# Token blocks 3 and 4 of the first MLP computed as a Strassen pair; the planned order extended through the first stage of the second MLP

## Chip, cores and metric

One core of a Trainium2 chip runs the whole program. The metric is device time in microseconds (us) of one execution, the median of the runs shown; beside it stands one execution under the profiler, from which all durations come.

## The reference

```python
q_s = softmax of q over its last axis; k_s = softmax of k over the sequence
kv = einsum('bhsd,bhse->bhde', k_s, v)          # 8 batches, 8 heads, 576 positions, width 64
x  = einsum('bhsd,bhde->bhse', q_s, kv)         # -> 4608 tokens x 512
x  = relu(x @ w_in) ** 2 @ w_out                # first MLP, 512 -> 2048 -> 512
out = (silu(x @ w_gate) * (x @ w_val)) @ w_out2 # second MLP, 512 -> 1536 -> 512
```

q, k and v are float32; the five weight matrices come as float64 and are turned into float32 words on the chip. Every product is made from two-part operands (a rounded part and the rest), three matmuls of 128x128 by 128x512 for one (`mm3`, line 104, whose matmul is line 107).

## The kernel before

The 4608 tokens are nine blocks of 512, numbered 0 to 8. **Direct blocks** (0 to 4, `NE = 5`) go through the first MLP with all eight quarter products of a block matrix product: 16 slices of the hidden width, each four `mm3` into a bank `ph`, the square of the relu, and four `mm3` into banks `acc`: 128 `mm3`, 384 matmuls a block. **Pairs** of blocks, here (5,6) and (7,8), use a seven-product Strassen scheme (`PRODUCTS`) in which the two blocks are the two halves of the rows: 672 matmuls a pair, in two halves, each of two `in_part`s (first weight) and one `out_part` (second weight). The sums on the operand side cost VectorE (DVE) and ScalarE (ACT) work that direct blocks do not have. The second MLP uses the same scheme in `groups` of two blocks (0,1), (2,3), (4,5), (6,7) and a half-width one for block 8: `gated` (504 matmuls a group) and then `out_stage` (252).

**Weight operands.** Pairs and groups read sums of weight quarters from DRAM (`hd`, `ad` for the first MLP; `gvd`, `od` for the second), 512 KB a load, through five slots (`Stream`; line 891 is the load). Two generators, `lane_one` and `lane_two`, make them: 16 "first sets" from words already converted (`first_sets`), then 18 "second sets" (`second_sets`): six gate, six val, then six out, each with two loads of 512 KB, the conversion of two halves (lines 399 to 409), quarter sums (line 334), and stagings (`staged`; line 297 on ACT, line 299 on DVE) with stores at line 326 of seven quarters of 256 KB. Quarters that need no sum are copied from the direct blocks' operands (`first_copies`, 48 stores).

**Attention** of block i, head pair hp is one unit (`kv_unit`, `q_unit`); from block 2 on its result goes to DRAM (`x1d`, store at line 731) and is loaded by `x_unit` (direct) or `bring` (pairs). There are 28 units from block 2 on.

**Order.** Block 0 follows a list written out by hand. Then `Plan`, a list scheduler with a cost for each step, writes every engine's instruction order: a step has an engine, a duration, needs, slots that it takes and frees, and a rank; where several could start on an engine, the lowest rank goes first. Ranks: tails of parts 0 to 0.9, chunks 1, operands `bring` 1.2, attention 2, matmuls of the main line (`direct`, `pair_main`) 3, stores and loads set aside by the lanes (`aside`) 4.9, the lanes 5, copies 6. Attention's unit j may start at 4 + 16j (k, v) and 12 + 16j (q) of planned time (`PACE = 16.0`). The plan runs to the end of the pairs, until the operands of the first group and all second sets are planned; behind it come the eight banks of the second MLP and its ordinary program order, in which each load into a slot is issued from SyncE (SP) when the matmuls ask for the slot.

Of the kernel before, what the change touches and what calls it, by code (L numbers as in the profile page):

```python
# [22 lines left out]
def tile_linear_attention_two_mlps(  # L23
# [45 lines left out]
    ps_a = st_att.enter_context(tc.tile_pool(name="ps_a", bufs=2, space=PSUM))  # L69
# [21 lines left out]
    NE = 5  # L91
# [104 lines left out]
    class Plan:  # L196
# [45 lines left out]
        def run(self, until):  # L242
            while not all(x in self.done for x in until):
# [18 lines left out]
        def finish(self, rank):  # L262
            for u in self.units:
                if u[0] == rank:
                    for _ in u[1]:
                        pass
# [6 lines left out]
    def aside(steps):  # L273

        if prep["plan"]:
            plan.unit(steps, 4.9, plan.now)
        else:
            yield from steps

    made = set()  # L280
    prep = {"n": 0, "issue": nc.sync, "plan": True}

    def aside(steps):

        if prep["plan"]:
            plan.unit(steps, 4.9, plan.now)
        else:
            yield from steps

    made = set()  # L290
    prep = {"stages": [(stp, "wst")] + [(raws, "raw0"), (raws, "raw1")], "raws": [], "n": 0, "r": 0}
    prep.update(issue=nc.sync, plan=True, last={})
# [8 lines left out]
    def staged(place, source, dests, by_rows=False, free=(), key=None):  # L301
# [3 lines left out]
        prep["n"] += 1  # L305
        keep = (tag, prep["n"])
# [16 lines left out]
        def put():  # L323
            yield step("SP", 0.6 * k_, done, (), [keep], [key] if key else (), 4.0)
            for j, to in enumerate(dests):
                prep["issue"].dma_start(to, f32(t[0][:, j]))

        yield from aside(put())
# [29 lines left out]
    class Lane:  # L358


        def __init__(self, halves, raw, stages):
            self.halves, self.raw, self.stages = halves, raw, stages
            self.n = 0

# [4 lines left out]
        def load(self, s, x):  # L369
            kind, f = s  # L370
            tag, tile_ = self.halves[x]
            yield step("SP", 0.6, (), [(tag, s)] if tag else (), (), [("ld", s, x)], 4.0)
            self.loaded[s, x] = tile_()
            nc.sync.dma_start(self.loaded[s, x], w1d[kind[:-1]][f][:, x])
# [5 lines left out]
        def load_raw(self, s, x):  # L380
# [4 lines left out]
            yield step("SP", 0.8, (), [keep], (), [("ld", s, x)], 4.5)  # L385
# [28 lines left out]
        def first_sets(self):  # L414
# [3 lines left out]
            while s:  # L418
# [12 lines left out]
                for x, (source, names) in enumerate(todo):  # L431
# [4 lines left out]
                    if more and self.halves[1][0]:  # L436
                        yield from aside(self.load(more, x))
                if more and not self.halves[1][0]:
                    yield from aside(self.load_two(more))
                made.add(s)  # L440
# [3 lines left out]
        def second_sets(self):  # L444
# [4 lines left out]
            while s:  # L449
                kind, f = s  # L450
# [3 lines left out]
                yield from aside(self.load_raw(s, 1))  # L454
# [15 lines left out]
                if more:  # L470
                    yield from aside(self.load_raw(more, 0))
# [12 lines left out]
                made.add(s)  # L484
# [24 lines left out]
    def lane_two():  # L509
# [6 lines left out]
        lane = Lane(  # L516
            [("qs", q_spare), ("qs", q_spare)], "raw1",
            [slot(qtp, "qT1"), ("kvs", lambda: kv_slot)],
        )
        yield from lane.second_sets()  # L520

    lanes = [lane_one(), lane_two()]
    work = (x for steps in lanes for x in steps)
# [118 lines left out]
    def kv_unit(j, i, hp):  # L642
        me = ("kv", j)
        yield step("SP", 0.7, [("kt.", j - 1)] + ([("x", 1, 3)] if j == 1 else []), [("kt", j)], (), [("kt.", j)], 3.5, True)
# [47 lines left out]
    def v_unit(j, i, hp):  # L692
        yield step("SP", 1.2, (), [("vt", j)], (), [("vt.", j)], 4.0)
        load_v(i, hp)

    def q_unit(j, i, hp):
        n = len(list(runs(i)))
        needs = [("qs.", j - 1)] + ([("ld", 0, 1, "b21")] if j == NP * NE else [])
        yield step("SP", 1.2 * n, needs, [("qs", j)], (), [("qs.", j)], 3.5, True)
# [26 lines left out]
        if hp % 2:  # L726
            nc.vector.tensor_copy(e, px)
        else:
            nc.scalar.copy(e, px)
        yield step("SP", 0.6, (), (), [("e", me)], [("x1", i, hp)], 4.0)  # L730
        nc.sync.dma_start(x1d[i][:, hp], e)

    def q_rest(i, hp, slot, j):

        me = ("pq", i, hp)
        yield step("PE", 0.55, (), [("pa", me)], [("qs", j)])
# [9 lines left out]
        yield from parts(make, pt, (), [("qT", j)] if slot == 0 else (), [("pa", me)], (), (0.6, 0.7))  # L746
# [19 lines left out]
    def x_unit(i, hp):  # L766
# [4 lines left out]
        yield step("SP", 0.6, needs, [(home, me)], (), [("xl", i, hp)], 4.0, True)  # L771
# [22 lines left out]
    def x2_unit(i, d):  # L794
# [16 lines left out]
        yield step("SP", 0.6, (), (), [("e", me)], [("x2d", i, d)], 4.0)  # L811
# [37 lines left out]
    def copies_unit():  # L849
        steps = first_copies()  # L850
        for _ in range(6 * NM):
            yield step("SP", 0.6, (), (), (), (), 2.5, True)
# [4 lines left out]
    pools = {}  # L857

    class Stream:
# [34 lines left out]
        def fill(self):  # L894
            while self.free and len(self.slots) < len(self.todo):
                for need in self.todo[len(self.slots)][1]:
                    while need not in made:
                        next(work, None)
                self.fetch()

        def planned(self):
            for n in range(self.n_pairs + 4):
                needs = [("st", *x, y) for x in self.todo[n][1] for y in range(2)]
                if n < WS:
                    kind, f = w1.order[XS + n]
                    needs.append(("h", NE - 1, f) if kind == "in" else ("a", NE - 1, f, NP - 1))
                yield step("SP", 0.6, needs, [("slot", n)], (), [("wu", n)], 5.0)
# [89 lines left out]

    def wide(pool):
        return pools[pool].tile([P, 2, T], F32, name=pool, tag=pool)

    def bring(i, j, tiles, src, c, key, xkey, gone, first=()):
# [4 lines left out]
        for (name, b, d), (pool, tile_) in zip(at, tiles):  # L1006
            keys[name] = pool, (key, c, name)
            yield step("SP", 0.6, [(src[0], b, d) for _, b, d in at] + [*first], [keys[name]], (), [("ld", key, c, name)], 4.0)
# [155 lines left out]
    def out_part(k, p, half, ops):  # L1164
# [45 lines left out]
        def put(name, to, names_):  # L1210
            yield step("SP", 0.6, (), (), [key(name)], names_, 4.0)
# [44 lines left out]

    def half_sum(p, name, keep, n):
        yield step("SP", 0.6, [("pd", p, name)], [keep], (), [("end", p, name)], 4.0)
# [64 lines left out]
    def gated(g, f, xo):  # L1323
# [4 lines left out]
        def product(name, ps, start):  # L1328
# [7 lines left out]
            if g == 0:  # L1336
                for _ in range(6):
                    next(work, None)
# [386 lines left out]
```

## Time and profile before

| | |
|---|---|
| median of 3 runs | 1680.19 us (1680.05 to 1680.38) |
| profiled execution | 1678.33 us, span 1676.6 us |
| TensorE (PE) busy | 1632.3 us, 97% of the span |
| DVE, ACT, POOL busy | 1132.4 (68%), 902.8 (54%), 252.5 us (15%) |
| mean granted TensorE clock | 0.997 of full |
| DMA | 420 MB, 251 GB/s on average |

Stages of the profiled execution, by the first matmuls of each: direct block 1 begins at 129.3 us, block 3 at 344.2, the first pair at 553.9, the second at 716.9, the first stage of the second MLP at 880.8 and its out stage at 1009.9; group 1 runs its first stage from 1067.0 to 1181.3. Matmuls are pipelined, so a duration of 390 ns stands for a distance of some 0.23 us between starts; stretches of the span and counts say more than the busy share.

### The profile page before, as it was taken

How to read it: one execution, taken by the hardware profiler on the slowest of the kernel's cores; microseconds unless marked ns; L12 is line 12 of the kernel's file. 1: busy time of each engine (PE TensorE's matmuls, PEld its weight loads, DVE VectorE, ACT ScalarE, POOL GpSimd, SP SyncE). 2: the span in 40 equal slices, each digit the busy share in tenths (PEclk: the TensorE clock that was granted, in tenths of full speed). 3: DMA queues.
4: the chain of work that ended last, by engine and by line, in shares of the span. 5: the costliest groups of instructions: out<-in, count | busy, mean ns of one | idle time of the engine just before them, and what ended most of it. 6: DMA issues, size and time to landing. Idle time of an engine off the chain costs nothing.

```text
span 1676.6 us, 23953 instructions
## 1 busy us (share of the span) xinstructions
PE 1632.3 (97%) x8210; PEld 1340.4 (80%) x8210; DVE 1132.4 (68%) x1951; ACT 902.8 (54%) x1552; POOL 252.5 (15%) x234
## 2 busy tenths in 40 slices
PE   6999999999999999999997999999999999999998
PEld 4777887877888877777775888888888888888898
DVE  8877667667767777888785458544864476447646
ACT  7775555555656676677764336333633354335334
POOL 4871111111101200000000111011102110120020
PEclk9999999999999999999998999999999999999999
DMA  9968779866656899899986678867686768666897
GB/s 298 292 184 246 246 242 276 275 201 184 197 162 192 275 317 378 303 341 336 357 312 216 199 215 272 253 191 222 215 247 192 217 216 247 196 204 201 258 386 261
DMA packets 275018, 420.00 MB, mean 251 GB/s; under 512 B 126288, under 2 KB 167248, under 8 KB 274896
## 3 DMA queue, kind: packets, MB, share of 16 engines
q1 hardware_dynamic: 274352, 418.33, 78.1%
q8 instruction: 66, 1.08, 0.3%
q14 instruction: 56, 0.46, 0.1%
q10 hardware_dynamic: 544, 0.13, 0.0%
HBM read 317.19 MB, written 101.19 MB: 250 GB/s over the span
## 4 chain that ended last, share of the span: by engine, by line
PE 83%; DMA 4%; DVE 4%; ACT 2%; issue 1%; SPq 1%; POOL 0%; DVEq 0%; ACTq 0%; POOLq 0%
PE ps L107 59%; PE ph L107 11%; PE acc L107 10%; PE pa L619 1%; DMA wu<-hd 1%; DMA od<-wst 1%; PE pa L107 1%; DVE wst L299 1%; PE pa L740 1%; DMA gvd<-wst 0%; DVE wsum L334 0%; DMA w<-in_moe_w_out_dram 0%; ACT wst L297 0%; DVE uo L1159 0%; ACT u L1113 0%
## 5 line engine op out<-in xcount | busy, mean ns | idle before, releaser
L107 PE MATMUL ps<-w,wu 128*128 128x512 f32 (+1 forms) x3192 | 678.7, 374 | 16.8 <-DMA wu<-gvd 10.5
L107 PEld LDWEIGHTS ps<-w,wu 128*128 128x128 f32 x3192 | 565.4, 189 | 126.4 <-issue 10.9
L107 PE MATMUL ps<-uo,wu 128*128 128x512 f32 (+1 forms) x1932 | 419.2, 378 | 2.0 <-DVE uo L1159 1.9
L107 PEld LDWEIGHTS ps<-uo,wu 128*128 128x128 f32 x1932 | 344.9, 188 | 74.7 <-DVE uo L1159 5.6
L107 PE MATMUL ph<-xT,w 128*128 128x512 f32 x960 | 246.7, 400 | 1.1 <-ACT xT L297 0.6
L107 PE MATMUL acc<-g,w 128*128 128x512 f32 x960 | 245.8, 399 | 0.8 <-DVE g L1571 0.8
L107 PEld LDWEIGHTS ph<-xT,w 128*128 128x128 f32 x960 | 175.9, 188 | 42.1 <-ACT xT L297 0.9
L107 PEld LDWEIGHTS acc<-g,w 128*128 128x128 f32 x960 | 175.8, 188 | 40.5 <-DVE g L1571 1.2
L1345 DVE TENSOR_TENSOR u<-u,ps 128x512 f32<-128x512 f32 (+1 forms) x60 | 38.0, 633 | 213.9 <-ACT u L1344 213.9
L101 ACT CAST uo<-u 128x512 fp32r<-128x512 f32 (+1 forms) x210 | 120.0, 579 | 114.0 <-DVE u L1346 41.8
L1350 POOL TENSOR_TENSOR u<-u 128x512 f32<-128x512 f32 (+1 forms) x30 | 35.3, 1178 | 948.0 <-DVE u L1346 948.0
L102 DVE TENSOR_TENSOR uo<-u,uo 128x512 fp32r<-128x512 f32 (+1 forms) x210 | 133.2, 651 | 32.3 <-ACT uo L101 31.9
L1297 ACT COPY ps<-ps 128x512 f32<-128x512 f32 x126 | 72.0, 572 | 134.3 <-PE ps L107 133.0
L299 DVE TENSOR_TENSOR g<-r,g 128x512 fp32r<-128x512 f32 x64 | 46.5, 726 | 87.1 <-ACT g L297 87.0
L1159 DVE TENSOR_TENSOR uo<-u,uo 128x512 fp32r<-128x512 f32 x112 | 73.5, 686 | 15.0 <-ACT uo L1157 15.0
L1157 ACT CAST uo<-u 128x512 fp32r<-128x512 f32 x112 | 66.8, 620 | 28.1 <-PE ps L107 27.7
L297 ACT CAST wst<-wsum 128x512 fp32r<-128x512 f32 (+1 forms) x88 | 58.5, 666 | 37.5 <-DVE wsum L409 18.4
L784 ACT ACTIVATE r<-ph 128x512 f32<-128x512 f32 x64 | 38.2, 597 | 73.3 <-PE ph L107 72.7
L706 POOL TENSOR_TENSOR qs<-qs,qm 128x512 f32<-128x512 f32 x28 | 30.9, 1103 | 305.2 <-DVE qm L704 185.8
L299 DVE TENSOR_TENSOR wst<-wsum,wst 128x512 fp32r<-128x512 f32 (+1 forms) x88 | 66.1, 753 | 7.9 <-ACT wst L297 6.6
L1344 ACT ACTIVATE u<-ps 128x512 f32<-128x512 f32 (+1 forms) x60 | 33.3, 555 | 55.3 <-PE ps L107 55.3
L1306 ACT COPY p<-ps 128x512 f32<-128x512 f32 x63 | 36.9, 587 | 44.8 <-PE ps L107 44.2
(193 smaller groups left out, 1747.4 us busy)
## 6 DMA issues: line engine op xcount, KB each, us to landing
wu<-gvd SPq DMA_DIRECT2D x210, 512.0 KB, 4.4
wu<-od SPq DMA_DIRECT2D x105, 512.0 KB, 4.4
wu<-hd SPq DMA_DIRECT2D x56, 512.0 KB, 6.3
wu<-ad SPq DMA_DIRECT2D x56, 512.0 KB, 5.7
gvd<-wst SPq DMA_DIRECT2D x76, 256.0 KB, 3.9
od<-wst SPq DMA_DIRECT2D x36, 256.0 KB, 4.1
w<-in_moe_w_in_dram SPq DMA_DIRECT2D x16, 512.0 KB, 6.9
w<-in_moe_w_out_dram SPq DMA_DIRECT2D x16, 512.0 KB, 6.7
```

Of the source, the lines that this page charges most:

```text
L101: nc.scalar.copy(hi, src)
L102: (eng or nc.vector).tensor_tensor(lo, src, f32(hi), op=ALU.subtract)
L107: nc.tensor.matmul(ps, lhsT=w[s], rhs=x[t], start=start and n == 0, stop=stop and n == 2, skip_group_check=more,)
L297: nc.scalar.copy(hi, src)
L299: nc.vector.tensor_tensor(lo, src, f32(hi), op=ALU.subtract)
L784: nc.scalar.activation(r, ph, AF.Relu)
L1157: nc.scalar.copy(t[:, 0], src())
L1159: nc.vector.tensor_tensor(t[:, 1], src(), f32(t[:, 0]), op=ALU.subtract)
L1297: nc.scalar.copy(x, y)
L1306: nc.scalar.copy(x, y)
L1345: nc.vector.tensor_tensor(u, u, gate, op=ALU.mult)
L1350: nc.gpsimd.tensor_tensor(s1, a21, a22, op=ALU.add)
```

## The change

`NE` becomes 3: blocks 0 to 2 stay direct, and (3,4), (5,6), (7,8) are pairs. Attention is spaced by 13 up to block 4, 15.5 for blocks 5 and 6, and 20 for 7 and 8; the copy of its result is always on ACT. The copies get rank 4.8 and a shorter planned time, a slot of the last direct weights waits for them too (`w_gone`), and planned costs of SP steps become smaller. A lane stops before a new second set once product 1 of the last pair's last `in_part` is done, until the second MLP's pools are open; then it goes on, with other buffers, beside the first stage of group 0. That stage is now planned (`gated_main`, `gated_part`): banks two wide in the manner of `in_part`, its three sums on DVE instead of POOL, its slot loads at planned places. Group 0's out stage and all later groups stay as they were, but the loads for the next group's operands begin with group 0's out stage.

```diff
-    NE = 5
+    NE = 3
...
+        def at_rest(self, token):
+            return all(token in u[2][2] for u in self.units if u[0] == 5) and not any(
+                u[0] == 4.9 and u[2][4] for u in self.units
+            )
...
         def second_sets(self):
...
             while s:
+                if self.stop in plan.done and "second MLP" not in plan.done:
+                    yield step("DVE", 0.02, ["second MLP"])
...
-        engine = "DVE" if hp % 2 else "ACT"
-        yield step(engine, 0.65, (), [("e", me)], [("pa", me)])
+        yield step("ACT", 0.6, (), [("e", me)], [("pa", me)])
...
-            yield step("SP", 0.6, (), (), (), (), 2.5, True)
+            f, x = divmod(n, 6)
+            names = [("copied", ("in", "out")[x // 3], f)] if x % 3 == 2 else ()
+            yield step("SP", 0.5, (), (), (), names, 1.9, True)
...
+    def w_gone(kind, f):
+        last = ("h", NE - 1, f) if kind == "in" else ("a", NE - 1, f, NP - 1)
+        return [last, ("copied", kind, f % NM)]
...
-            for n in range(self.n_pairs + 4):
+            for n in range(self.n_pairs + 7 * NG + 4):
...
+    def gated_part(k, f, ops):
+        xo = pair_x[-1]
...
+                yield step("PE", 1.361, need, take, [("slot", slot)] if kind else ())
...
+                for j in range(NP // 2):
+                    wj = u[:, 0, j * P:(j + 1) * P], u[:, 1, j * P:(j + 1) * P]
+                    mm3(two_banks[k, bank][:, kind], wj, xo.of[name][j], start and j == 0, j == 1, True)
...
+        def post(name):
...
+                yield step("DVE", 1.22, [("p5", k)], [key(name)], (), [("ev22", k)])
...
+            yield step("ACT", 0.6)
+            u = us[name] = tile_of("u", "u")
+            nc.scalar.activation(u, x[:, 0], AF.Sigmoid)
+            yield step("DVE", 0.66)
+            nc.vector.tensor_tensor(u, u, x[:, 0], op=ALU.mult)
+            yield step("DVE", 0.66, (), (), [free], [("u", k, name)])
+            nc.vector.tensor_tensor(u, u, x[:, 1], op=ALU.mult)
+            if name == "12":
+                plan.unit(sums(), 0.5)
...
+    def gated_main(k, ops):
+        for f in range(NG):
+            yield from gated_part(k + f, f, ops)
...
-        plan.unit(copies_unit(), 6, 12.0)
+        plan.unit(copies_unit(), 4.8, 12.0)
...
-        PACE = 16.0
         units = [(i, hp) for i in range(2, NB) for hp in range(NP)]
+        at = 4.0
         for j, (i, hp) in enumerate(units):
             if i < B:
-                plan.unit(kv_unit(j, i, hp), 2 + j / 100, 4.0 + PACE * j)
-            plan.unit(q_unit(j, i, hp), 2 + j / 100, 12.0 + PACE * j)
+                plan.unit(kv_unit(j, i, hp), 2 + j / 100, at)
+            plan.unit(q_unit(j, i, hp), 2 + j / 100, at + 8.0)
+            at += 13.0 if i < NE + 2 else 15.5 if i < NE + 4 else 20.0
...
+            plan.run(["end of pairs"])
+            plan.run(lambda: plan.at_rest("second MLP"))
+            st_first.close()
+            st_att.close()
...
+            lane_b.halves = [half_slot("wb2"), half_slot("wb3")]
...
+            plan.done["second MLP"] = plan.now, None
+            first = []
+            plan.unit(gated_main(3 * 2 * len(pairs), first), 3)
             plan.run(
-                ["end of pairs"] + [("xo", len(pairs), n, c) for n in PRODUCTS for c in range(NP // 2)]
-                + [("wu", stream.n_pairs + 3)]
+                [("gated", f) for f in range(NG)] + [("wu", stream.n_pairs + 7 * NG + 3)]
+                + [("st", kind, f, x) for kind, f in sets for x in range(2)]
             )
-            plan.run([("st", kind, f, x) for kind, f in sets for x in range(2)])
-            plan.finish(4.9)
...
+            if g == 0:
+                ops = first
+                after = second_x(g + 1)
+                after.load(0)
+            for f in range(NG) if g else ():
                 ops.append(gated(g, f, xo))
```

## Rows read from the trace of the kernel before

**Rows 1.** TensorE groups, whole span: xcount, busy us, mean ns, idle before.

```profile
L107 PE MATMUL ph<-xT,w 128*128 128x512 f32 x960 | 246.7, 400 | 1.1 <-ACT xT L297 0.6 <-DVE xT L1549 0.3 <-DVE xT L299 0.2
L107 PE MATMUL acc<-g,w 128*128 128x512 f32 x960 | 245.8, 399 | 0.8 <-DVE g L1571 0.8
```

**Rows 2.** stretches: length; busy PE, PEld, DVE, ACT, POOL (count); clock; DMA share; GB/s.

```profile
129.30:344.20 214.90, 212.51 (x1238) 169.72 (x1237) 149.63 (x320) 123.49 (x226) 29.36 (x26) 1.00 0.84 257
344.20:553.90 209.70, 207.17 (x1171) 167.49 (x1169) 148.09 (x297) 125.45 (x229) 25.88 (x23) 1.00 0.63 188
553.90:716.90 163.00, 160.69 (x703) 129.55 (x703) 126.94 (x193) 108.85 (x155) 8.10 (x7) 1.00 0.93 326
716.90:880.80 163.90, 158.57 (x676) 125.42 (x674) 134.71 (x192) 117.01 (x159) 0.00 (x0) 1.00 0.94 336
880.80:1009.90 129.10, 117.17 (x505) 96.06 (x504) 71.24 (x108) 50.99 (x82) 19.28 (x15) 0.96 0.67 209
1067.00:1181.30 114.30, 114.30 (x506) 94.62 (x505) 55.27 (x86) 42.49 (x72) 19.29 (x15) 1.00 0.71 216
```

**Rows 3.** chain that ended last, 179 to 191 us: start, us, what.

```profile
179.39 0.44 PE pa L740 x4
183.73 0.86 PE pa L107 x6
190.30 0.85 PE pa L619 x24
```

**Rows 4.** attention's TensorE groups inside 344.2:553.9 (direct blocks 3 and 4).

```profile
L107 PE MATMUL pa<-qT,kv 128*128 128x320 f32 (+5 forms) x72 | 11.6, 297 | 0.0
```

**Rows 5.** timeline of TensorE behind the pairs: start, us, what.

```profile
904.24 8.14 PE L107 MATMUL ps<-w,wu 128*128 128x512 f32 x25 [10.54 <-DMA wu<-gvd]
```

**Rows 6.** timeline of SyncE's DMA queue at the same place.

```profile
899.04 0.79 SPq L326 DMA_DIRECT2D od<-wst  x2
899.93 9.86 SPq L891 DMA_DIRECT2D wu<-gvd  x6
```

**Rows 7.** two short stretches after that: length, busy PE (count), clock, DMA share.

```profile
904.20:909.10 4.90, 4.86 (x12) 0.51 0.86 351
909.10:914.00 4.90, 4.90 (x23) 1.00 0.52 134
```

**Rows 8.** VectorE groups in 553.9:880.8, the two pairs.

```profile
L1159 DVE TENSOR_TENSOR uo<-u,uo 128x512 fp32r<-128x512 f32 x112 | 73.5, 686 | 15.0 <-ACT uo L1157 15.0
L1129 DVE TENSOR_TENSOR u<-ps,u 128x1024 f32<-128x1024 f32 x16 | 19.5, 1217 | 2.2 <-PE ps L107 2.2
L299 DVE TENSOR_TENSOR w<-x,w 128x512 fp32r<-128x512 f32 x23 | 15.8, 686 | 1.9 <-ACT w L297 1.9
L299 DVE TENSOR_TENSOR wst<-wsum,wst 128x512 fp32r<-128x512 f32 (+1 forms) x29 | 22.6, 780 | 4.0 <-ACT wst L297 3.7
L334 DVE TENSOR_TENSOR wsum<-wsum 128x256 f32<-128x256 f32 x28 | 12.7, 455 | 0.7
L409 DVE SCALAR_TENSOR_TENSOR wsum<-wraw,wsum 128x512 int32<-128x512 int32 x16 | 11.0, 686 | 0.3
```

**Rows 9.** VectorE groups, whole span.

```profile
L299 DVE TENSOR_TENSOR g<-r,g 128x512 fp32r<-128x512 f32 x64 | 46.5, 726 | 87.1 <-ACT g L297 87.0
L727 DVE COPY e<-pa 128x512 f32<-128x512 f32 x14 | 9.6, 683 | 0.5 <-PE pa L107 0.5
L1346 DVE TENSOR_TENSOR u<-u,ps 128x512 f32<-128x512 f32 (+1 forms) x60 | 38.0, 633 | 4.9 <-PE ps L107 0.5
```

**Rows 10.** timeline of SyncE's DMA queue near 340.

```profile
335.23 1.36 SPq L326 DMA_DIRECT2D ad<-wst  x2
339.99 0.33 SPq L731 DMA_DIRECT2D x1d<-e  x1
346.59 0.43 SPq L117 DMA_DIRECT2D wraw<-in_moe_w_gate_dram  x1
```

**Rows 11.** the page, part 2: GB/s in 40 slices of the span.

```profile
GB/s 298 292 184 246 246 242 276 275 201 184 197 162 192 275 317 378 303 341 336 357 312 216 199 215 272 253 191 222 215 247 192 217 216 247 196 204 201 258 386 261
```

More of the change, by code (lines that the diff above doesn't have):

```diff
@@ L242, in run @@
         def run(self, until):
-            while not all(x in self.done for x in until):
+            while not (until() if callable(until) else all(x in self.done for x in until)):
                 todo = [(s, u) for u in self.units for s in (self.start(u),) if s is not None]
@@ L273, in aside @@
     def aside(steps):
[L275 to L292, printed above, removed]
+        plan.unit(steps, 4.9, plan.now)
+    n_staged = [0]
     def parts(make, src, needs=(), take=(), free=(), names=(), d=(0.6, 0.68)):
@@ L323, in put @@
         def put():
-            yield step("SP", 0.6 * k_, done, (), [keep], [key] if key else (), 4.0)
+            yield step("SP", 0.5 * k_, done, (), [keep], [key] if key else (), 4.0)
             for j, to in enumerate(dests):
-                prep["issue"].dma_start(to, f32(t[0][:, j]))
-        yield from aside(put())
+                nc.sync.dma_start(to, f32(t[0][:, j]))
+        aside(put())
     def quarter_sums(m, n, by_rows):
@@ L371, in load @@
             tag, tile_ = self.halves[x]
-            yield step("SP", 0.6, (), [(tag, s)] if tag else (), (), [("ld", s, x)], 4.0)
+            yield step("SP", 0.5, (), [(tag, s)] if tag else (), (), [("ld", s, x)], 4.0)
             self.loaded[s, x] = tile_()
@@ L436, in first_sets @@
                     if more and self.halves[1][0]:
-                        yield from aside(self.load(more, x))
+                        aside(self.load(more, x))
                 if more and not self.halves[1][0]:
-                    yield from aside(self.load_two(more))
-                made.add(s)
+                    aside(self.load_two(more))
                 s = more
@@ L453, in second_sets @@
                 yield from self.bits(s, 0)
-                yield from aside(self.load_raw(s, 1))
+                aside(self.load_raw(s, 1))
                 m = self.loaded.pop((s, 0))
@@ L470, in second_sets @@
                 if more:
-                    yield from aside(self.load_raw(more, 0))
+                    aside(self.load_raw(more, 0))
                 n = self.loaded.pop((s, 1))
@@ L515, in lane_two @@
         yield step("DVE", 0.02, [("raw1", keys[-1]) for keys in (plan.pools["raw1"][1],)])
[L516 to L520, printed above, removed]
+        lane_b.halves = [("qs", q_spare), ("qs", q_spare)]
+        lane_b.raw = "raw1"
+        lane_b.stages = [slot(qtp, "qT1"), ("kvs", lambda: kv_slot)]
+        yield from lane_b.second_sets()
     lanes = [lane_one(), lane_two()]
-    work = (x for steps in lanes for x in steps)
     def first_to(kind, f, name):
@@ L643, in kv_unit @@
         me = ("kv", j)
-        yield step("SP", 0.7, [("kt.", j - 1)] + ([("x", 1, 3)] if j == 1 else []), [("kt", j)], (), [("kt.", j)], 3.5, True)
+        yield step("SP", 0.5, [("kt.", j - 1)] + ([("x", 1, 3)] if j == 1 else []), [("kt", j)], (), [("kt.", j)], 3.5, True)
         kt = None
@@ L692, in v_unit @@
     def v_unit(j, i, hp):
-        yield step("SP", 1.2, (), [("vt", j)], (), [("vt.", j)], 4.0)
+        yield step("SP", 1.0, (), [("vt", j)], (), [("vt.", j)], 4.0)
         load_v(i, hp)
@@ L735, in q_rest @@
         me = ("pq", i, hp)
-        yield step("PE", 0.55, (), [("pa", me)], [("qs", j)])
+        yield step("PE", 0.55, (), [("pa", me)] + ([("qT", j)] if slot == 0 else []), [("qs", j)])
         pt = pa_tile()
@@ L744, in make @@
             return t[:, 0], t[:, 1]
-        yield from parts(make, pt, (), [("qT", j)] if slot == 0 else (), [("pa", me)], (), (0.6, 0.7))
+        yield from parts(make, pt, (), (), [("pa", me)], (), (0.6, 0.7))
     def new_x(i, hp):
@@ L1007, in bring @@
             keys[name] = pool, (key, c, name)
-            yield step("SP", 0.6, [(src[0], b, d) for _, b, d in at] + [*first], [keys[name]], (), [("ld", key, c, name)], 4.0)
+            yield step("SP", 0.5, [(src[0], b, d) for _, b, d in at] + [*first], [keys[name]], (), [("ld", key, c, name)], 4.0)
             made_[name] = tile_()
@@ L1210, in put @@
         def put(name, to, names_):
[L1211 removed]
+            yield step("SP", 0.5, (), (), [key(name)], names_, 4.0)
             nc.sync.dma_start(to, ends[p, half, name])
@@ L1679, in tile_linear_attention_two_mlps @@
             if g == 0:
-                for _ in work:
-                    pass
                 st_prep.close()
```

137 lines of the change are left out of this document (91 added, 46 removed).

## The prediction, made before the changed kernel was built

> **What bounds the kernel now.** I read the stretches first, one per stage, and in each compared the count of matmuls with its length. TensorE starts a full matmul about every 0.23 us and has little else to wait for. Group 1's first stage is the cleanest example: 504 matmuls in 114.3 us, 0.2268 us each, clock 1.00, busy in all of it [rows 2]. So the time is the number of matmuls times that distance, plus what each stage loses. A direct block is 960 + 960 matmuls over five blocks, 384 each [rows 1], or 87.1 us at 0.2268; a pair has 672, or 152.4 us. The pairs lose most: the second took 163.9 us [rows 2], 11.5 over clean, a factor of 1.076, with VectorE (DVE) busy 134.7 us of it (82%) and the DMA engines at 0.94. Group 0's first stage took 129.1 us for what group 1 does in 114.3, 14.8 more [rows 2]. The timeline shows most of that: TensorE stood 10.54 us for a load from `gvd` [rows 5], which SyncE issued only at 899.93, behind the last stores of second sets [rows 6]; then the granted clock was 0.51, the 1.2 GHz level, for 4.9 us, with 12 matmuls where the next 4.9 us at full clock hold 23 [rows 7]: 11 x 0.227 = 2.5 us more.
>
> **Term 1, direct blocks 3 and 4 become a pair.** They occupy 209.7 us [rows 2], in which TensorE also does attention: 72 matmuls of six per unit [rows 4], so 12 units, each 0.86 (x sums) + 0.85 (kv sums) + 0.44 us (transposes) in the chain [rows 3]: 12 x 2.15 = 25.8 us, which is moved, not removed. 209.7 - 25.8 = 183.9 us is replaced by a pair at the measured price, 163.9: -20.0 us. Small transposes of some 0.1 us that I did not count could make it -18; the count alone, 96 matmuls fewer at 0.2268, gives -21.8. I take -20.
>
> **Term 2, group 0's first stage is planned.** The loads from `gvd` get places between the stores instead of behind them, so the 10.54 us and the slow clock after it should go. Best end: group 1's length, 114.3, or -14.8 us. The new stage, however, is no longer alone: it works beside what is left of the second sets, in banks two wide and with three sums more on DVE. Per part that is two wide adds of 1.22 [rows 8], eight multiplications of 0.633 [rows 9], three sums of about 0.64 and a split of 0.69 (estimates from the rows of like size): 2.4 + 5.1 + 1.9 + 0.7 = 10.1 us of DVE, 61 us for six. A second set costs DVE about 8.5 us: four stagings of 0.78, four quarter sums of 0.455, and two conversions of 2 x 0.686 + 0.42 [rows 8], the 0.42 an estimate for one cheap step. Five left over make 43, together 104 of 120 us, as dense as a pair. The pairs' factor gives 114.3 x 1.076 = 123, or -6. I take 120 us, -9, between the ends, since DMA is lighter there (0.67 against 0.94 [rows 2]).
>
> **Term 3, the same side work in less time.** A pair's DVE work: 56 chunk splits of 0.686, 32 wide operations of 1.22, 14 operand splits and 8 sums of 0.69 [rows 8]: 38.4 + 39.0 + 15.1 = 92.5 us. A direct block has 16 splits of 0.726 [rows 9] and six small ones of 0.69: 15.7. The 14 copies moved to ACT free 14 x 0.683 = 9.6 [rows 9]; ACT has room (117 of 163.9 in the second pair [rows 2]), so they cost nothing unless attention's chain waits for ACT. Net +92.5 - 31.4 - 9.6 = +51.5 us. From 129.3 to 880.8 DVE was busy 149.6 + 148.1 + 126.9 + 134.7 = 559 of 751.5 us, 74% [rows 2]; afterwards 611 of about 741, 82%: the densest stretch of before, now as the mean. Five sets moved behind the pairs bring it to 77%. DMA: the rates times the lengths [rows 2] make 55 + 39 + 53 + 55 = 203 MB; a pair adds 56 loads of 0.52 MB and 4 MB of half sums, 33 MB. Less five sets of 2.9 MB that is 222 MB in 741 us, 300 GB/s, and 317 from the first pair on, just below the pairs of before. Both resources stay under what they have sustained, but the first two pairs now have attention of blocks 5 to 8 beside them. Attention outranks the lanes, so first the sets yield; price between 0 and a doubled loss of 11.5 us in two pairs (+23). I take +4 for each, nearer to the low end because the first pair of before held the last attention units and still took 163.0. One more us for blocks 1 and 2, where attention runs closer.
>
> **Edits at no cost.** The copies' higher rank puts 48 stores ahead of the lanes' stores on SyncE's queue; all first sets were stored at 335 [rows 10], 200 us ahead of the pairs, now about even with them, but only half of them are needed for the first half. If that cover is gone it is a wait of one set, some 10 us (200 us for 16 sets gives 12.5 each). The hold on the lanes emits no instruction; it queues nothing on DVE and costs sets, below. Three sums leave POOL, which waits on nothing then. The next group's operand loads are issued later, when group 0's out stage begins, with TensorE's first product there (36 matmuls, 8 us) as cover; uncovered, 5 us.
>
> **Sum.** -20 - 9 + 8 + 1 = -20 us. The profiled execution took 1678.33 us (span 1676.6, 1.7 around it), so 1658.3; the median was 1.9 higher: 1660.
>
> **Rivals.** (a) *Second sets late*, the slower side. Out-stage operands need all six out sets within its first product, and with them unfinished TensorE stands at the stage's start. Before, 18 sets took from 346.6 [rows 10] to 899.8 [rows 6], 30.7 us each. Now they start later, at about 370 (attention denser, first pair's operands made in the same stretch), and stop for some 57 us before the pairs' end (the rest of an `in_part`, 17, and an `out_part`, 40): up to the first stage's end, about 870 + 120 = 990, that is 563 us, or 18.3 sets at the old pace. There is no margin at that pace. For it: DVE is fuller than before. Against: in the new stage DVE is half free for them. It decides if more than one set is open at the end; three open are 3 x 8.5 + 2.5 for the slower clock = 28 us: 1688. (b) *DVE or DMA congestion* in the first two pairs takes +22 rather than +8: 1674. The Trainium skill, "DMA: Bandwidth & Descriptors", section Specifications, puts the HBM limit of a core at about 358 GB/s, which would leave the pairs of before, at 336, without reserve; one slice of the page shows 378 and another 386 GB/s [rows 11], so the trace does not bear it out as a ceiling, and I hold this rival lower than the rule alone would put it. (c) *The first pair waits for x.* Its last attention unit, number 11, was stored at 340.0 [rows 10] at a spacing of 16; at 13 it is 33 us earlier, 307; loads (an estimate of 5 us) and a chain of seven splits and four sums (12 us by the rows of like size) end at 324, and blocks 1 and 2 end near 344. If the spacing cannot be kept, they end at 357 and 13 to 16 us go: 1676. Then the change does not do what it says, attention being what sets the pace. (d) *No new loss*: -21.8 - 14.8 = -36.6, or 1644.
>
> **How the numbers follow.** The forecast (1650 to 1670) has 0.50, (d) 0.16, (b) 0.14, (c) 0.06, (a) 0.14. A change under 0.2% (3.4 us) could not be told from none. Faster: 0.50 + 0.16 + 0.10 of (b) + 0.03 of (c) = 0.79; same 0.04 + 0.03 = 0.07; slower 0.14. The range 1646 to 1682 leaves out (a) and the best of (d).
>
> **What would show it.** 672 matmuls between direct block 2 and the old first pair, near 165 us; no stop of 10 us at the begin of the second MLP and no clock of 0.51 there; DVE at 80% or more in all three pairs; group 0's first stage between 114 and 123 us. Wrong if TensorE stops at the first pair for x, at group 0's out stage for loads from `od`, or if a pair takes over 175 us.

## The result, and the profile after

The changed kernel takes 1659.36 us (median of 4 runs, 1653.84 to 1660.42) against 1680.13 for the kernel before: a ratio of 0.9869, 95% interval 0.9847 to 0.9892, or 20.8 us less where 20 were forecast. Its profiled execution took 1660.13 us, with a span of 1658.3. The four runs differ by 0.4%, those of the kernel before by 0.02%.

The stretches of the changed kernel, one per stage: direct blocks 1 and 2, the three pairs, then group 0's first stage and its out stage. Columns as in [rows 2].

```profile
129.00:248.10 119.10, 113.13 (x676) 89.54 (x676) 85.76 (x184) 67.84 (x126) 17.44 (x16) 0.99 0.93 285
248.10:358.00 109.90, 106.63 (x649) 85.25 (x647) 82.94 (x175) 69.20 (x129) 12.89 (x11) 1.00 0.84 261
358.00:547.40 189.40, 183.79 (x991) 148.92 (x990) 151.05 (x254) 126.94 (x197) 28.23 (x24) 0.98 0.94 287
547.40:710.10 162.70, 160.97 (x701) 129.50 (x700) 130.37 (x193) 111.64 (x161) 6.68 (x6) 1.00 0.93 327
710.10:873.10 163.00, 158.24 (x673) 126.61 (x672) 129.88 (x192) 110.53 (x157) 0.00 (x0) 0.99 0.95 340
873.10:990.90 117.80, 116.17 (x507) 94.56 (x506) 103.64 (x156) 62.49 (x83) 0.00 (x0) 1.00 0.90 312
990.90:1049.00 58.10, 57.63 (x253) 47.37 (x254) 50.71 (x83) 32.24 (x58) 0.00 (x0) 1.00 0.86 285
```

The span of the profiled execution fell by 18.3 us, from 1676.6 to 1658.3. By stage, against [rows 2] and the stage borders of the kernel before, that is:

| stage | before | after | difference |
|---|---|---|---|
| blocks 1 and 2 | 214.9 | 229.0 | +14.1 |
| blocks 3 and 4 with two pairs / three pairs | 536.6 | 515.1 | -21.5 |
| group 0, first stage | 129.1 | 117.8 | -11.3 |
| group 0, out stage | 57.1 | 58.1 | +1.0 |

Group 1's first stage took 114.3 us before and 114.2 after; of the other 0.5 us, 0.3 lie ahead of block 1, the rest behind group 1. The count of TensorE instructions in blocks 1 and 2 rose from 1238 to 676 + 649 = 1325: some 87 instructions, or 2.4 attention units at 36 each, were moved forward into them. At 2.15 us a unit [rows 3] that is 5.2 of the 14.1 us (an estimate); 8.9 are loss. By the columns of busy time, TensorE stood idle for 9.2 us in these two blocks, where it stood for 2.4 before [rows 2]: 6.9 of the 8.9 us. The other 2.0 us are busy time beyond the moved attention.

At the place of the old 10.54 us stop [rows 5] TensorE's timeline now shows this, and SyncE's queue below it has the loads from `gvd` between other transfers, where [rows 6] had them behind the last stores:

```profile
873.13 3.60 PE L108 MATMUL ps<-w,wu 128*128 128x512 f32 x15
877.68 0.50 PE L108 MATMUL ps<-w,wu 128*128 128x512 f32 x1 [0.94 <-ACT w L283]
878.40 5.95 PE L108 MATMUL ps<-w,wu 128*128 128x512 f32 x25 [0.22 <-DVE w L285]
```

```profile
881.20 0.32 SPq L312 DMA_DIRECT2D od<-wst  x1
883.42 0.33 SPq L116 DMA_DIRECT2D wraw<-in_moe_w_out_dram  x1
883.85 0.38 SPq L879 DMA_DIRECT2D wu<-gvd  x1
```

The stage no longer runs alone: DVE works 103.6 of 117.8 us in it, where it worked 71.2 of 129.1 before, since five second sets are still to be made and the three sums of a part have come to it from POOL (19.3 us there before, none now). How many sets were done when it began can be read from the stores issued between 129 and 873.1 us (count, KB each, us to landing), seven a set:

```profile
gvd<-wst SPq DMA_DIRECT2D x72, 256.0 KB, 5.5
gvd<-kv SPq DMA_DIRECT2D x12, 256.0 KB, 6.9
od<-wst SPq DMA_DIRECT2D x7, 256.0 KB, 6.8
```

That is 91 stores, 13 sets of 18. The last stores were issued 5.5 us ahead of the out stage, as SyncE's timeline shows:

```profile
985.37 0.80 SPq L312 DMA_DIRECT2D od<-o  x2
```

### The profile page after: what moved, and what is told of

Read it like the earlier page. It is cut to its first block, busy times and chain, and to the rows that moved or that the text cites. A ratio compares the mean times of both kernels' runs of the same rounds, so it can differ in the third digit from the quotient of the medians.

```text
span 1658.3 us, 23943 instructions
## 1 busy us (share of the span) xinstructions
PE 1615.5 (97%) x8114; PEld 1326.5 (80%) x8114; DVE 1191.3 (72%) x2009; ACT 928.5 (56%) x1561; POOL 230.7 (14%) x216
## 4 chain that ended last, share of the span: by engine, by line
PE 78%; DMA 6%; DVE 6%; ACT 2%; issue 1%; SPq 1%; POOL 0%; DVEq 0%; ACTq 0%; POOLq 0%
PE ps L108 66%; PE ph L108 5%; PE acc L108 5%; DMA kt<-in_k_dram 1%; PE pa L604 1%; PE pa L108 1%; DMA wraw<-in_moe_w_val_dram 1%; DMA qs<-in_q_dram 1%; DMA x<-x2d 1%; DMA wu<-ad 1%; DMA gvd<-wst 1%; PE pa L721 1%; SPq L595 0%; DMA wraw<-in_moe_w_gate_dram 0%; DMA w<-in_moe_w_out_dram 0%
## 5 line engine op out<-in xcount | busy, mean ns | idle before, releaser
L108 PE MATMUL ps<-w,wu 128*128 128x512 f32 (+1 forms) x3528 | 762.8, 377 | 6.8 <-ACT w L283 2.6
L108 PEld LDWEIGHTS ps<-w,wu 128*128 128x128 f32 x3528 | 628.4, 189 | 129.9 <-DVE u L1123 3.5
L108 PE MATMUL ps<-uo,wu 128*128 128x512 f32 (+1 forms) x2268 | 500.1, 381 | 1.9 <-DMA wu<-ad 0.9
L108 PEld LDWEIGHTS ps<-uo,wu 128*128 128x128 f32 x2268 | 407.2, 188 | 89.1 <-DVE uo L1153 2.5
L108 PE MATMUL acc<-g,w 128*128 128x512 f32 x576 | 149.4, 402 | 4.8 <-ACT g L283 2.1
L108 PE MATMUL ph<-xT,w 128*128 128x512 f32 x576 | 148.3, 400 | 1.1 <-ACT xT L283 0.6
L108 PEld LDWEIGHTS acc<-g,w 128*128 128x128 f32 x576 | 106.0, 190 | 30.0 <-ACT g L283 3.0
L108 PEld LDWEIGHTS ph<-xT,w 128*128 128x128 f32 x576 | 105.7, 188 | 26.6 <-ACT xT L283 0.9
L1366 ACT COPY ps<-ps 128x512 f32<-128x512 f32 x102 | 58.1, 570 | 114.6 <-PE ps L108 113.6
L320 DVE TENSOR_TENSOR wsum<-wsum 128x256 f32<-128x256 f32 x124 | 58.0, 469 | 10.7 <-DMA wsum<-w1d_in 5.7
L1107 ACT ACTIVATE u<-u 128x1024 f32<-128x1024 f32 x48 | 51.0, 1061 | 1.5
```

What stands on the lines that cost most here:

```text
L108: nc.tensor.matmul(ps, lhsT=w[s], rhs=x[t], start=start and n == 0, stop=stop and n == 2, skip_group_check=more,)
L320: nc.vector.tensor_tensor(to, x, y, op=op)
L1107: nc.scalar.activation(u, u, AF.Square)
L1366: nc.scalar.copy(x, y)
```

## The experiments

All start from the changed kernel, and their stretches are cut at their own stage borders. Times are medians; each ratio is to the kernel before, run on the same chip.

**The planned stage without the pair.**

```diff
-    NE = 3
+    NE = 5
...
-        plan.unit(copies_unit(), 4.8, 12.0)
+        plan.unit(copies_unit(), 6, 12.0)
...
-            at += 13.0 if i < NE + 2 else 15.5 if i < NE + 4 else 20.0
+            at += 16.0
```

The x copies alternate between ACT and DVE again, and `w_gone` no longer waits for the copies.

> Blocks 3 and 4 stay direct (NE = 5, attention every 16, copies at rank 6 and on both engines as before); only the planned first stage of the second MLP, with the hold on the lanes, is kept. My theory: the two halves of the gain add up, so this gives term 2 alone, 129.1 us of the first stage falling to 114 to 118, and 129.3 to 880.8 stays at 751 +- 3: 1668 us. Rival: the planned stage pays only because the pair crowds out the sets; then the sets are nearly done at the pairs' end here too and the gain is the 10.5 us stop and the slow clock alone: also 1667, but with the first stage at 114.3 and DVE in it under 65%. Second rival: the hold of 57 us costs sets that then run late, 1675 or more.

Measured: 1686.28 us, ratio 1.0038 (1.0025 to 1.0051). The expectation was wrong, and so was its second rival in its mechanism: no set was late, the last store was issued at 831 us. The two pairs and the first stage:

```profile
559.00:724.50 165.50, 161.00 (x702) 129.28 (x702) 128.90 (x189) 110.18 (x156) 7.46 (x7) 1.00 0.92 318
724.50:890.60 166.10, 159.04 (x674) 127.53 (x673) 130.62 (x181) 113.31 (x149) 0.00 (x0) 0.98 0.90 316
890.60:1014.50 123.90, 118.54 (x508) 95.43 (x506) 66.16 (x90) 39.50 (x55) 0.00 (x0) 0.99 0.65 195
```

The stage gained 5.2 us, but blocks 1 to 4 took 429.2 instead of 424.6 us and the pairs 331.6 instead of 326.9, and the out stages of groups 0 and 1 lost 2.8. So the gains of the change are not two terms that add: the planned order with its other SyncE costs loses more ahead of the stage than it wins in it as long as there are five direct blocks. Which of its edits costs the 9.3 us ahead was not separated; what the trace shows is that the sets came sooner (831 against 899 us), in stages where they are beside the main line. The planned stage itself took 123.9 us with no set left to make beside it: TensorE stood 3.0 us for its operands near the beginning, and the clock was 0.62 in the 3.8 us after that.

**The pair without work beside the stage.**

```diff
-                if self.stop in plan.done and "second MLP" not in plan.done:
+                if False:
...
-            plan.run(["end of pairs"])
+            plan.run(["end of pairs"] + [("st", kind, f, x) for kind, f in sets for x in range(2)])
```

> Three pairs as changed, but the lanes are not held and the planned first stage waits until all second sets are planned, as before the change. My theory: at the pairs' end, 873 us in the changed kernel, five sets are open; without the hold about two more would be done, so three are left with TensorE standing for them, at 8.5 us of DVE each and more in latencies: 25 to 50 us of stop, a slow clock behind it, then 114 to 118 us for the stage: 1685 to 1710 us. That would show that the pair pays only with work going on beside the first stage. Rival: the lanes speed up enough without the hold and the stop is under 15 us: 1665 to 1672.

Measured: 1710.16 us, ratio 1.0178 (1.016 to 1.0195), the upper end of the theory. First TensorE's timeline, then two stretches with busy TensorE, granted clock, DMA share and GB/s:

```profile
924.66 5.52 PE L108 MATMUL ps<-w,wu 128*128 128x512 f32 x13 [42.31 <-ACT ps L1055]
```

```profile
882.20:924.60 42.40, 0.15 (x1) 0.54 0.69 251
924.70:929.00 4.30, 4.30 (x10) 0.50 0.87 275
```

TensorE stands for 42 us while the five sets are made, and pays a slow clock after it. One detail was wrong: 13 sets were stored by 873 us here too, so by then the hold had cost no whole set. In this order the pair pays only because the sets may go on beside the first stage; without that the kernel is slower than before.

**Later planned landings.**

```diff
-            yield step("SP", 0.5, (), [(tag, s)] if tag else (), (), [("ld", s, x)], 4.0)
+            yield step("SP", 0.5, (), [(tag, s)] if tag else (), (), [("ld", s, x)], 7.0)
...
-            yield step("SP", 0.55, (), [keep], (), [("ld", s, x)], 4.5)
+            yield step("SP", 0.55, (), [keep], (), [("ld", s, x)], 9.0)
```

The reason for trying it is the one long stop of the changed kernel, in its first pair. The chain of work there:

```profile
458.58 9.03 DMA wraw<-in_moe_w_val_dram
...
467.63 0.67 ACT wsum L386
...
470.12 0.95 DVE kt L653
...
471.10 0.85 ACT kt L659
```

and the timelines of ACT and TensorE, with what ended their idle time:

```profile
467.63 0.66 ACT L386 ACTIVATE wsum<-wraw 128x512 f32<-128x512 f32 x1 [5.57 <-DMA wraw<-in_moe_w_val_dram]
472.00 1.68 PE L604 MATMUL pa<-vt,kt 96*64 96x65 f32 x24 [4.49 <-ACT kt L659]
```

A raw weight load planned at 4.5 us landed after 9.0. Its reader, an instruction of a lane, whose rank comes last, stood at the head of ACT's queue for 5.6 us; attention's next steps came behind it, and TensorE waited 4.5 us for them.

> The changed kernel with other planned landing times for the lanes' loads: 4.0 becomes 7.0 (words) and 4.5 becomes 9.0 (raw weights); nothing else. My theory of the loss in blocks 1 and 2 (some 9 us over before) and in the first pair: instructions of the lanes stand at the head of the ACT and DVE queues for loads that land later than planned, and attention and the main line queue behind them, up to TensorE. Then the stops of 4.9 us near 467 and of 4 us near 242 go and the time falls by 5 to 10 us, to 1650 to 1655. Rival (the engines are simply full, or attention is too close): no change, 1657 to 1661, or slower because sets come later.

Measured: 1696.79 us, ratio 1.0093 (1.0079 to 1.0107). Blocks 1 and 2 took 229.3 us, as before the edit, and the first pair 190.6. The edit did reach the waits: DVE waited 8.2 us for the lanes' words in blocks 1 and 2 of the changed kernel and does not here, and the stop of 4.5 us in the first pair is gone, with others of 2.1 and 2.3 us in its place. So late loads of the lanes alone are not what blocks 1 and 2 lose. What the edit also did is hold up the sets: only 65 + 12 stores, 11 sets, by 873.1 us, and the slower rival of the prediction came true at the beginning of the out stage:

```profile
gvd<-wst SPq DMA_DIRECT2D x65, 256.0 KB, 5.6
gvd<-kv SPq DMA_DIRECT2D x12, 256.0 KB, 6.0
```

```profile
1029.87 4.50 PE L108 MATMUL ps<-uo,wu 128*128 128x512 f32 x10 [29.07 <-DMA wu<-od]
```

**Attention at 16 throughout.**

```diff
-            at += 13.0 if i < NE + 2 else 15.5 if i < NE + 4 else 20.0
+            at += 16.0
```

> The changed kernel with attention every 16 for all units, as before the change. Rival (c) of the prediction: the first pair waits for x, 13 to 16 us lost against the change: 1672 to 1676. My theory now, since blocks 1 and 2 ended only at 358 in the changed kernel: block 4's last unit at 340 plus 17 us for the operands comes at 357, so little is lost there, and blocks 1 and 2 get 3 to 5 us back by fewer units and fewer stops; later attention goes into the second and third pair: 1657 to 1664.

Measured: 1677.52 us, ratio 0.9984 (0.9972 to 0.9996): the time of rival (c), not its mechanism. Blocks 1 and 2 fell to 219.8 us and the first pair began at 349, sooner than in the changed kernel; 25 us were lost behind it, in the three pairs (532.3 instead of 515.1 us, of which some 5 are attention left over) and the first stage (125.9 instead of 117.8):

```profile
349.30:544.70 195.40, 185.90 (x1026) 148.93 (x1025) 156.40 (x267) 130.15 (x203) 23.54 (x20) 0.97 0.93 282
544.70:712.30 167.60, 165.47 (x755) 133.86 (x754) 134.48 (x210) 115.69 (x171) 13.39 (x12) 1.00 0.92 315
712.30:881.60 169.30, 160.32 (x673) 128.12 (x672) 130.96 (x193) 110.26 (x156) 0.00 (x0) 0.97 0.91 320
```

The third pair has no more attention on TensorE than before the edit (673 instructions in both) and still takes 6.3 us more. The longest stops are waits for the operands `w` near the beginning of a stage: 3.0 us in the first pair, 3.9 in the third, 5.7 in the first stage; the changed kernel has none, 1.7 and 0.9 there.

The run also splits the 14.1 us of blocks 1 and 2. With 1237 TensorE instructions, as many as before the change, they took 4.9 us more than before. The closer spacing adds the 5.2 us of moved attention and 4.0 us of loss.

**SyncE's durations as measured.** In the changed kernel SyncE issued 72% of the time between 129 and 345 us, with 0.62 us for a load of q, 0.70 for v, 0.65 for a copy.

```diff
-        yield step("SP", 1.0, (), [("vt", j)], (), [("vt.", j)], 4.0)
+        yield step("SP", 1.4, (), [("vt", j)], (), [("vt.", j)], 4.0)
...
-        yield step("SP", 1.0 * n, needs, [("qs", j)], (), [("qs.", j)], 3.5, True)
+        yield step("SP", 1.25 * n, needs, [("qs", j)], (), [("qs.", j)], 3.5, True)
...
-            yield step("SP", 0.5, (), (), (), names, 1.9, True)
+            yield step("SP", 0.65, (), (), (), names, 1.9, True)
```

> The changed kernel with planned SyncE durations as the traces show them: 1.25 instead of 1.0 for two loads of q (four issues of 0.62 for a usual unit), 1.4 instead of 1.0 for the two of v, 0.65 instead of 0.5 for a copy; the change had lowered these. New theory: in blocks 1 and 2 SyncE's issue queue runs behind the plan (72% issuing; back to back from 224 to 261), so loads of k and of the lanes' words are issued late, DVE and ACT stand for them, and TensorE loses the 9 us. Then blocks 1 and 2 fall from 229 to 220 to 224 us and the time to 1650 to 1655. Rival (DVE and ACT are full, or the attention's chain is too long): 229 stays, 1657 to 1661. Late second sets would show as a stop at 991.

Measured: 1674.71 us, ratio 0.9974 (0.9962 to 0.9985). The stretches of blocks 1 and 2 and of the first pair:

```profile
130.90:242.00 111.10, 108.40 (x638) 86.51 (x637) 79.77 (x170) 65.08 (x119) 15.23 (x14) 1.00 0.92 285
242.00:353.70 111.70, 107.75 (x674) 85.75 (x672) 79.89 (x173) 69.41 (x130) 12.38 (x11) 1.00 0.81 247
353.70:538.80 185.10, 182.72 (x1000) 147.80 (x1000) 144.15 (x251) 126.12 (x196) 28.56 (x24) 1.00 0.97 293
```

222.8 instead of 229.0 us, as expected, and 4.3 less in the first pair. The second half of the expectation failed. The later pairs took 166.4 and 171.1, 11.8 us more; by the end of the pairs 12 sets were stored, one fewer; and the out stage began with a stop:

```profile
1005.66 6.60 PE L108 MATMUL ps<-uo,wu 128*128 128x512 f32 x16 [8.34 <-DMA wu<-od]
```

**Copies from GpSimd's queue.**

```diff
-            yield step("SP", 0.5, (), (), (), names, 1.9, True)
+            yield step("POOL", 0.5, (), (), (), names, 1.9, True)
...
-                    nc.sync.dma_start(first_to(kind, f, name), f32(t[:, :, c:c + U]))
+                    nc.gpsimd.dma_start(first_to(kind, f, name), f32(t[:, :, c:c + U]))
```

> The changed kernel with the 48 copies issued from GpSimd's queue instead of SyncE's, nothing else. By the queue theory 31 us of issuing leave SyncE in blocks 1 and 2 (216 us), and these fall from 229 to 220 to 224 us: 1650 to 1656. Against it, two attention steps run on GpSimd and may wait behind an issue. Rival (total DMA traffic is what costs, 285 GB/s in block 1): nothing changes but the order, 1656 to 1662.

Measured: 1660.52 us, ratio 0.9881 (0.9866 to 0.9895), not to be told from the change. SyncE's issuing fell from 72% to 63%, but blocks 1 and 2 took 115.3 + 114.2 = 229.5 us. So a lighter SyncE queue alone does not give them back what they lose (GpSimd's own issuing may have taken some of a gain away; no run separates that), and e5's gain there came from another order, since SyncE has the same transfers to issue in e5 as in the changed kernel. The first pair of e6, however, has no stop of 4.5 us:

```profile
360.10:540.60 180.50, 179.57 (x985) 145.54 (x983) 140.97 (x242) 124.35 (x191) 25.12 (x22) 1.00 0.97 295
```

It takes 8.9 us less than the changed kernel's and has a clock of 1.00 instead of 0.98, which bears out what that stop costs. The next two pairs (169.0 and 165.0 us, 8.3 more together) gave the gain back.

**Less DVE work.** The quarter sums of the weight operands are left out, so this kernel's output is not the reference's.

```diff
         def tt(to, x, y, op):
-            nc.vector.tensor_tensor(to, x, y, op=op)
+            pass
```

> The changed kernel with the quarter sums of the weight operands left out (four DVE instructions of 0.45 in each of the 34 sets, 62 us of DVE), plan and order as they are. If full DVE is what costs TensorE its time, blocks 1 and 2 (16 sets, 29 us less DVE) fall by 5 us or more, and the three pairs by 3 each: 1645 to 1650. By the queue theory DVE was waiting for loads anyway: under 4 us in all, 1655 to 1659.

Measured: 1656.82 us, ratio 0.9859 (0.9847 to 0.9872). Blocks 1 and 2:

```profile
130.30:249.40 119.10, 113.70 (x676) 90.81 (x676) 72.03 (x149) 68.22 (x127) 17.63 (x16) 0.97 0.93 289
249.40:358.20 108.80, 106.50 (x648) 85.17 (x647) 71.43 (x146) 68.46 (x128) 13.21 (x11) 1.00 0.84 260
```

DVE is busy 143.5 us instead of 168.7 in them, and they are 1.1 us shorter; the whole kernel's 2.5 us lie within the spread of the changed kernel's own runs. The stop in the first pair is still 4.1 us. DVE's fill, on which term 3 of the prediction was worked out, is not what TensorE waits for there.

**Copies behind the lanes.** `plan.unit(copies_unit(), 6, 12.0)` instead of 4.8.

> The changed kernel with the copies back at rank 6, behind the lanes, as before the change. By the queue theory the copies leave block 1, which falls from 119 to 112 or less, and go to block 2, where they may hold up the first pair's slots: 1655 to 1662. If rank makes no difference (the copies are hidden anyway), block 1 stays at 119.

Measured: 1675.04 us, ratio 0.997 (0.9959 to 0.9981). Block 1 fell to 114.8 us, blocks 1 and 2 to 226.7, but 12 sets were stored by 873 us, the first stage took 124.3 us and the out stage 69.4, with a stop of 8.5. So the copies' rank, which the prediction put among the edits at no cost, is worth some 16 us here, all of it in these two stages, where it lets the lanes finish in time.

**Three tries for both gains.** The measured SyncE durations, or the copies on GpSimd with the durations of q and v, each with attention of blocks 7 and 8 at 15.5, so that lane two starts sooner; and that spacing alone.

```diff
-            at += 13.0 if i < NE + 2 else 15.5 if i < NE + 4 else 20.0
+            at += 13.0 if i < NE + 2 else 15.5
```

> As e5_sp_costs, with attention of blocks 7 and 8 spaced by 15.5 instead of 20, so that the last unit, which lane two awaits before its second sets, comes some 30 us sooner. Theory: e5 gained 8.6 us up to the end of the first pair and gave back more because the second sets came late (8.7 us stop in group 0's out stage). With lane two earlier the stop goes and the gain stays: 1650 to 1660. Rival: the second and third pair pay for the denser attention, and the sets are held by SyncE and ACT, not by lane two's start: 1665 to 1675, stop at the out stage still there.

> Copies from GpSimd's queue (e6), planned durations of the q and v loads as measured (e5), attention of blocks 7 and 8 at 15.5. If SyncE's queue is what the first stages lack, this has the shortest blocks 1 and 2 and first pair of all, 400 us or less in sum (418 in the changed kernel, 408 in e5), and, with sets in time, 1648 to 1656. If the sets are late again, 1660 to 1672 with a stop behind 990.

> The changed kernel with the one edit of attention at 15.5 for blocks 7 and 8. If late sets hang on lane two's start, the last store of second sets comes 15 us or more before 985.7, and the time stays (nothing waits there now): 1656 to 1662. If denser attention costs the pairs more than 3 us, 1662 to 1668.

Measured: 1705.3 us (ratio 1.0144, 1.0127 to 1.0161), 1674.94 (0.9967, 0.9955 to 0.9979) and 1669.7 (0.9934, 0.9919 to 0.9949). All three times lie outside what was expected. The slower branches for the second and the third named what happened (late sets; a denser attention that costs the pairs), but not its size. With 15.5 alone the last store came at 996, not sooner, and the pairs took 525.6 us, 10.5 more. In the first, 11 sets were stored by 873 us and the out stage had stops of 16.6 and 12.9 us; in the second, 12 sets and one of 8.7. Blocks 1 and 2 with the first pair took 420.1 us in the second, against 418.4: nothing won.

**The other way.** `24.0` in place of `20.0`.

> The changed kernel with attention of blocks 7 and 8 spaced by 24 instead of 20. In e11 the spacing of 15.5 cost the three pairs 12 us in sum; if crowding by attention is what they pay for, 24 gives them some 3 to 5 us back. Against it, lane two starts some 25 us later: 12 instead of 13 second sets stored by 873, which in e5 and e8 went with a stop of 9 us at group 0's out stage. Crowding alone: 1654 to 1657. Both: 1662 to 1668. If the order matters more than either, anything up to 1680.

Measured: 1674.3 us, ratio 0.9968 (0.9958 to 0.9978), neither of the two prices; it falls under the last clause, which names no mechanism. The third pair took 171.5 us with a stop of 4.3, and the first stage 125.9 with one of 5.7, both for the operands (`w`) of the stage. Ahead of each, a transfer planned at 4 to 4.5 us took longer again (two lines of the chain), and ACT waited for it (two lines of its timeline):

```profile
706.80 7.56 DMA wraw<-in_moe_w_gate_dram
878.78 8.22 DMA gvd<-wst
```

```profile
714.39 0.66 ACT L386 ACTIVATE wsum<-wraw 128x512 f32<-128x512 f32 x1 [0.68 <-DMA wraw<-in_moe_w_gate_dram]
887.08 0.62 ACT L283 CAST wst<-qs 128x512 fp32r<-128x512 f32 x1 [3.00 <-DMA gvd<-wst]
```

ACT's wait is 3.0 of the 5.7 us, but only 0.7 of the 4.3: the picture of the changed kernel's first pair comes again in the first stage, and hardly in the third pair, where ACT and DVE by turns make the operands.

No variant with the full output was faster than the changed kernel.

## Why the prediction was right, and where it was not

**Term 1**, -20 us for the pair in place of two direct blocks, holds as the sum of its parts: -21.5 us for the three pairs against [rows 2], of which 5.2 are attention that went ahead, so -16.3 of work and loss. With the +8 that term 3 put on the first two pairs the forecast was -12; against the -20 of the term alone the pairs cost 3.7 us more than the old price.

**Term 2**, -9 us, was -11.3: the stop and the slow clock went, and the stage took 117.8 us where 120 were forecast, 3.6 over group 1's 114.2 and less than the pairs' factor of 1.076 gave. These 3.6 us are not shown to be the price of the work beside it, since e1's planned stage took 123.9 with none. Nor is it a term of its own: e1 has the planned stage without the pair and is slower than before, and e2 has both but no sets beside the stage, and is slower still. The prediction's step of adding the two was right in size and, as far as e1 with its other edits can show, wrong in kind.

**Term 3** was too small and in the wrong place. +8 us were put on the first two pairs and +1 on blocks 1 and 2, 9 in sum. Measured, blocks 1 and 2 lost 8.9 us beside the attention moved into them, and the pairs 3.7, 12.6 in sum. The first pair lost most, some 18 us over clean: 189.4 - 152.4 for the matmuls, less 8.9 attention units (319 instructions beyond 672, at 36) of 2.15. The mis-sized step is the "one more us for blocks 1 and 2", which measured 8.9: by e4 4.0 us for the closer spacing and 4.9 for the other edits at the old spacing. The 5.2 us of moved attention come on top; they are no loss, only work in another place. And the resource was misnamed: e7 takes 25 us of DVE out of these blocks and 1.1 us of time goes. What the traces show at the longest stop, in the first pair, and in part at e12's later ones is an in-order queue whose head waits for a transfer that took 7.6 to 9 us instead of the planned 4 to 4.5. For the many small losses in blocks 1 and 2, no stop of which is longer than 1.4 us, no single cause was found: DVE's fill (e7), the lanes' load times (e3) and SyncE's load (e6) were each eased, and these blocks stayed within 1.1 us of 229. That stays open.

**The sum** is closer than its terms. Forecast and measured stand at +1 and +8.9 for blocks 1 and 2, -12 and -16.3 for the pairs, -9 and -11.3 for the first stage, 0 and +1.0 for the out stage. The errors largely cancel, so that the median came within a microsecond of the forecast is luck; the variants, from 1657 to 1710 us, show how far a single edit moves it.

**The signs.** The stop and the slow clock at the beginning of the second MLP are gone, the first stage lies between 114 and 123 us, and DVE is busy for 79.7 to 80.1% of each pair, as good as the 80% that the prediction named. One sign of being wrong came: a pair over 175 us. The first took 189.4, some 170 with its attention taken out, against the 165 that were named; the sign did not allow for attention in that pair, and the stop of 4.5 us was not foreseen.

**Rival (a)**, second sets late, was the nearest to coming true. The estimate of no margin was right: the last store comes 5.5 us ahead of the stage that reads it. Its price was near: 28 us were worked out for three open sets, and in e3, with 15 stores (two sets and one store of a third) still to be issued when the out stage began, TensorE stood for 29.1 and 2.9 us. With 5 or 6 stores to go (e5, e8, e10) it stood for 8.3 to 8.7 us. The count of 57 us of hold was too high: in the changed kernel DVE makes no set from 840 to 876 us, 36 us, and in e2, without the hold, it goes on at 857.

**Rival (b)**, congestion in the first two pairs, did not come in the pairs' sum: 3.7 us over the old price, where +22 were put. **Rival (c)** was right in the time of its trial (1676 forecast, 1677.5 in e4) by another way: the first pair waits only 3.0 us for its operands, and the rest is lost in the later stages, in part to the attention left over and in part at late operands. **The edit at no cost** whose cover was named, the loads at the beginning of the out stage, cost up to 1.0 us (58.1 against 57.1).

## What to carry to other kernels

Price an exchange of stages by what each takes in the trace with its side work taken out, and then ask which deadline the side work itself has: here the orders that shortened the early stages (e4, e5, e8) paid it back at late operands, some 8 to 9 us where one set was late and 29 to 32 where two were. A list scheduler's order is worth several us either way, so an edit that is good where it is aimed can lose in the whole (e5). An engine that is 74% busy, as DVE is in blocks 1 and 2, need not be the limit: take work off it and see, as e7 did.

## What the hardware showed that was not expected

Short stops cost more than their length. Three stretches of the changed kernel with the granted clock near half (busy TensorE with its count, clock, DMA share, GB/s):

```profile
243.30:246.70 3.40, 3.26 (x11) 0.56 0.73 219
472.00:478.80 6.80, 6.80 (x37) 0.53 0.93 299
717.80:721.10 3.30, 3.30 (x10) 0.55 1.03 394
```

The second follows the stop of 4.49 us before 472.00; ahead of the other two TensorE's timeline has two stops each, with one matmul between them:

```profile
242.04 0.50 PE L108 MATMUL acc<-g,w 128*128 128x512 f32 x1 [1.36 <-ACT g L283]
243.44 1.22 PE L108 MATMUL acc<-g,w 128*128 128x512 f32 x2 [0.90 <-DVE g L285]
715.37 0.50 PE L108 MATMUL ps<-w,wu 128*128 128x512 f32 x1 [1.66 <-ACT w L283]
716.49 1.76 PE L108 MATMUL ps<-w,wu 128*128 128x512 f32 x5 [0.63 <-DVE w L285]
```

Together that is 13.5 us near the 1.2 GHz level, and some 6 us lost, an estimate from the mean clock of 0.54. Two stops of 0.78 and 1.00 us near 258 had no such stretch behind them: the clock was 1.00 from 258.2 to 261.6. The Trainium skill, "TensorE: Matmul & The Clock Gate", section "Part 1: The HAM clock gate", has the clock at half rate after idle and full when busy; the trace agrees for the stop of 4.5 us and shows the drop also behind two stops of 0.6 to 1.7 us with a matmul between them.

The third pair moved 340 GB/s over 163 us, and 394 GB/s in the last of these stretches; [rows 11] had 386 in a slice of 42 us. The limit of some 358 GB/s that "DMA: Bandwidth & Descriptors" (the Trainium skill, section Specifications) gives for a core was exceeded in both; there the measurement decides. Copies issued from GpSimd's queue (e6) took its engine about 0.7 us each: 46.5 us in 57 instructions in block 1 against 17.4 in 16.
